# Causal-window attention feeding a mixture of experts: probability-times-V by quadrants, with its output over two PSUM banks and one cycle later

## The chip, the cores and the metric

The kernel runs on one core of a Trainium2 chip. Its time is the device time of one execution in microseconds. Five engines work side by side: TensorE (PE, with its weight loads listed apart as PEld), VectorE (DVE), ScalarE (ACT), GpSimd (POOL) and SyncE (SP), which issues most DMAs. PSUM is the memory that TensorE writes, in banks of 512 fp32 columns by 128 partitions.

## The reference

Eight sequences of 576 tokens with 8 heads of 64 go through attention in a window of 128 keys with a linear bias by head. Each token's 512 numbers then go to the one of eight experts that a gate picks.

```python
scores = scale * np.matmul(q, k.transpose(0, 1, 3, 2))
mask = (rel >= 0) & (rel < window)              # rel = query - key, window = 128
scores = np.where(mask, scores + bias[None], -1000000000.0)
attn = np.exp(scores - np.max(scores, axis=-1, keepdims=True))
attn = attn / (np.sum(attn, axis=-1, keepdims=True) + 1e-09)
x = np.matmul(attn, v)                          # then (B * S, H * D)
expert_idx = np.argmax(x @ w_gate, axis=1)
...
h = np.maximum(xe @ w1[e], 0.0)
out[mask] = gate_w[mask, None] * (h @ w2[e])
```

## The kernel before, in words

**Chunks.** Attention works on 36 chunks of 128 queries: four whole ones per sequence (m = 0 to 3) and, for each pair of sequences, one tail chunk made of the last 64 queries of both. A chunk with m > 0 sees two blocks of 128 keys, its own (kb = 1) and the one ahead (kb = 0). A chunk with m = 0 sees its own alone. In a tail chunk the own block has 64 keys. So there are 8 chunks with m = 0, 24 full ones and 4 tails.

**Steps of a chunk.** `scores` (S0 and S1, four heads each) adds the bias by a matmul and then the products of q and k, in 64*64 tiles of the array. Since each query sees 128 keys of 256, the two halves are folded by `copy_predicated` in `weigh` (F) and ACT takes the exponents (E0; E10 and E11 for the two halves of S1's). `transposes` (T0, T1) turns the probabilities into a bank of `b_ps`. `place` (P0, P1) copies that bank by ACT to `pT` at kb = 1 and then has POOL write kb = 0 and kb = 1 by `affine_select`, which sets to zero what the window leaves out. `av` (V0, V1) multiplies by v into a bank of `b_ps`; `copy_x` (X) copies that by ACT to `xT`. `rows` (R) turns the rows back and takes the gate's products. `scale_rows` (Y) divides by the sum and starts the write to DRAM.

**V.** Each matmul of `av` has a head's 64 columns of v as weights (128 keys) and 128 columns of `pT` as the moving operand. The masked `pT` holds two quadrants of zeros in each full chunk: late keys of the own block for the first 64 queries, and early keys of the block ahead for the last 64. V multiplies them too. Tiles are named rows*columns in the trace: 128*64 for V, and 64*64 for S and R.

**Order.** The order is written by hand. A cycle is four steps of `step(s)`; chunk ch starts at step 4*ch. `PLACES` gives each operation its step and its rank in the step. On PE a cycle is S0 of the newest chunk, T1 and T0 of older ones, R, S1 and V. V at (11, 7) is in the same cycle as T1 and P1 at 8 of its chunk. X stands at (11, 9), R at 16. Chunks outside `SPLIT` (the first ones) take the exponents of S1 in one piece and their sums on DVE (`SUMS`).

**Beside it.** While attention runs, 14 halves of expert weights are rounded to fp32r by ACT (`round_half`, a cast) and their rest is taken by POOL (`rest_half`). `W0` and `W1` say in which cycles, and when the halves are loaded. Loads are spread over slots, `PN` = 5 to a cycle, with a due slot and a first slot for each kind. `route` is a generator: each piece of routing a group of chunks is run at the end of a cycle.

**PSUM.** `ps_s` has four banks for scores, `ps_r` two for R, and `ps_b` two that rotate among T1, T0 and V.

Of the kernel before, what the change touches and what calls it, by code (L numbers as in the profile page):

```python
# [44 lines left out]
def attention(ctx, tc, st, qT, kT, v, iw, load_c2, chunk_done, chunks, begun):  # L45
# [7 lines left out]
    ptp = ctx.enter_context(tc.tile_pool(name="a_pt", bufs=2))  # L53
    xp = ctx.enter_context(tc.tile_pool(name="a_x", bufs=2))
    ps_s = ctx.enter_context(tc.tile_pool(name="ps_s", bufs=1, space=PSUM))
    ps_b = ctx.enter_context(tc.tile_pool(name="ps_b", bufs=2, space=PSUM))
    ps_r = ctx.enter_context(tc.tile_pool(name="ps_r", bufs=1, space=PSUM))
    st["bank"] = bank = lambda: ps_b.tile([128, 4, 128], F32, name="b_ps")
    flat = lambda ap: ap.rearrange("p a b -> p (a b)")
    st["ptp"] = ptp  # L60

# [184 lines left out]
    def av(subs, pT, x_ps, pairs):  # L246
        m, tail = subs[0][1] // 4, is_tail(subs)
        spans = [(subs[2 * a][0], slice(64 * a, 64 * a + 64)) for a in range(2)] if tail else [(subs[0][0], slice(0, 128))]
        whole = [(p, b, q, kb) for p in pairs for b, q in spans for kb in ((0, 1) if m > 0 else (1,))]
        if tail:  # L250
            whole.sort(key=lambda x: x[3])
        for p, b, q, kb in whole:
            kk = 64 if (m == 4 and kb == 1) else 128
            first, last = kb == 0 or m == 0, kb == 1
            if tail:
                first, last = (p, b, q, kb) == whole[0], (p, b, q, kb) == whole[-1]
            for c in range(2):
                h = 2 * p + c
                anchor(nc.tensor.matmul(  # L259
                    out=x_ps[64 * c:64 * c + 64, p, q], lhsT=blocks["v", b, m - 1 + kb][0:kk, D * h:D * h + D],  # L260
                    rhs=pT[0:kk, kb, h, q], start=first, stop=last,
                ))

    def rows(xT):
        st["r_ps"] = r_ps = ps_r.tile([128, 2, 512], F32, name="r_ps")
# [29 lines left out]
                        needs[key].append((j, ch))  # L295
                    uses[key][j] = ch
    wanted = []
    for key, load, have, bufs, free, due in (("q", load_q, 3, QBUF, 3, -2 * PN - LEAD[0]), ("v", load_v, 2, VBUF, 2 * PN + 4, 2 * PN + 3 - LEAD[1])):
# [40 lines left out]

    def copy_x(ch):  # L340
        xTs[ch] = xp.tile([128, NP, 128], F32, name="xT", bufs=3)
        nc.scalar.copy(out=xTs[ch], in_=xps.pop(ch))

    def do(k, ch):
        perform(k, ch)
# [3 lines left out]
    def perform(k, ch):  # L349
# [11 lines left out]
        elif k == "E10":  # L361
            weighed[ch, 1]((0,))
        elif k == "E11":
            weighed.pop((ch, 1))((1,))
        elif k in ("A0", "A1"):
            nc.vector.tensor_reduce(out=sums[ch][:, 4 * g:4 * g + 4], in_=pes[ch][:, 4 * g:4 * g + 4, :], axis=AX.X, op=ALU.add)
            if g:
                guard(sums[ch])
        elif k in ("T0", "T1"):
            if ch not in pTs:  # L370
                pTs[ch] = ptp.tile([128, 2, H, 128], F32, name="pT")
            turned[ch, g] = transposes(g, pes[ch])
# [55 lines left out]
    for s in range(HAND, max(plan) + 1):  # L428
        step(s)


SPLIT = range(3, 36)
SUMS = {0: (2, 6), 1: (4, 6), 2: (6, 6)}
PLACES = dict(S0=(0, 0), T1=(8, 1), E11=(4, 2), T0=(4, 3), P1=(8, 4), P0=(4, 5), R=(16, 6), F0=(0, 7), Y=(16, 8), S1=(0, 9),
              F1=(0, 10), E0=(0, 11), V0=(11, 7), V1=(11, 7.2), X=(11, 9), I=(15, 9.5), E10=(3, 10))
HOOKS = dict(Q=4.5, G=20, round=(2, 2), rest_of=(2, 21))
SLOTS = dict(S0=0, T0=1, S1=2, V0=3, V1=4)
PN = 5
LEAD = (7, 10, 11, 8)
# [113 lines left out]
def route(tc, st, lg, c0, G, groups):  # L553
# [875 lines left out]
```

## Time and profile before

| | us |
|---|---|
| time, median of 3 runs | 627.55 (626.51 to 627.57) |
| the profiled execution, its own time | 626.94 |
| its span, first to last instruction | 625.2 |
| PE busy in the span | 614.3 (98%) |
| attention at its steady pace, 20.86 to 192.42 | 171.56 |
| from there to the first steady expert work at 213.30 | 20.88 |
| the rest, expert work | 411.90 |

The page gives busy time of each engine over the whole span. The view by windows gives it by stretch. The timeline lists what each engine did in order, neighbours of one kind merged: start, length, engine, line, operation, what it writes and reads, the tile of the array, the operands' shape and the count, and in brackets the idle time ahead of it with what ended it. The length of a merged PE row reaches to the end of its last matmul, which overlaps the next row; so the distance between two starts is what a step costs.

### The profile page before, as it was taken

The page shows a single profiled execution, that of the slowest core. Times are in us where ns is not written, and L with a number is a line of the kernel's source. Part 1 is how long each engine was busy: PE and PEld are TensorE (multiplying, and loading weights), DVE is VectorE, ACT ScalarE, POOL GpSimd, SP SyncE. Part 2 cuts the span into 40 slices and gives each one's busy share as a digit, 9 for nine tenths or more (in the row PEclk, how much of TensorE's full clock was granted, in tenths as well). Part 3 has the DMA queues.
Part 4 walks back from the last instruction along what each step waited for, and adds up shares of the span by engine and source line. Part 5 has one row for each costly group of instructions (what it writes and reads, how often), then busy time and mean ns, then how long its engine had stood idle before and what let it go on. Part 6 is the DMA issues. An engine that isn't in the chain of part 4 may idle for free.

```text
span 625.2 us, 16743 instructions
## 1 busy us (share of the span) xinstructions
PE 614.3 (98%) x6544; PEld 527.0 (84%) x6544; DVE 377.0 (60%) x887; ACT 312.7 (50%) x939; POOL 316.6 (51%) x483
## 2 busy tenths in 40 slices
PE   8999999999999999999999999999999999999996
PEld 5888877877878888898989999989999998888885
DVE  6777887877888875535654564565466365455411
ACT  5888888998886324423342333334234333433311
POOL 5646788978664221365247508624751750670302
PEclk9999999999999999999999999999999999999999
DMA  7757978788645256273444425434442642544101
GB/s 272 217 188 232 292 208 270 234 265 258 212 129 181 77 163 213 85 289 113 147 156 120 127 84 178 123 112 144 132 136 77 203 114 68 194 126 139 67 1 62
DMA packets 46995, 100.16 MB, mean 160 GB/s; under 512 B 12149, under 2 KB 12405, under 8 KB 46914
## 3 DMA queue, kind: packets, MB, share of 16 engines
q1 hardware_dynamic: 38434, 77.85, 39.1%
q0 software_dynamic: 8336, 20.96, 11.7%
q8 instruction: 52, 0.85, 0.6%
q10 hardware_dynamic: 144, 0.26, 0.2%
q14 instruction: 29, 0.24, 0.1%
HBM read 78.96 MB, written 20.09 MB: 158 GB/s over the span
## 4 chain that ended last, share of the span: by engine, by line
PE 84%; POOL 7%; ACT 3%; DVE 2%; DMA 2%; issue 1%; POOLq 0%; DVEq 0%; ACTq 0%
PE y_ps L1037 32%; PE l_ps L831 31%; PE b_ps L259 7%; PE s_ps L192 4%; PE b_ps L227 3%; PE r_ps L271 2%; ACT pe L215 2%; POOL pT L243 2%; POOL wl L1154 2%; POOL pT L241 2%; PE s_ps L183 2%; PE s_ps L831 1%; POOL q_sb L86 1%; ACT pT L233 1%; PE x_ps L788 1%
## 5 line engine op out<-in xcount | busy, mean ns | idle before, releaser
L834 ACT ACTIVATE hh<-l_ps 128x320 fp32r<-128x320 f32 (+4 forms) x104 | 46.5, 447 | 200.8 <-PE l_ps L831 200.8
L838 DVE SCALAR_TENSOR_TENSOR hl<-l_ps,hh 128x320 fp32r<-128x320 f32 (+4 forms) x104 | 52.3, 502 | 146.9 <-ACT hh L834 146.6
L811 POOL DMA_INDIRECT xg<-xd,od_idx x112 | 116.4, 1039 | 35.1 <-issue 32.0
L1037 PE MATMUL y_ps<-wh,hh 128*128 128x512 f32 x280 | 109.9, 393 | 0.0
L1025 POOL DMA_INDIRECT out<-y,od_pidx x33 | 34.9, 1057 | 148.0 <-ACT y L1043 141.5
L1037 PE MATMUL y_ps<-wl,hh 128*128 128x512 f32 x280 | 109.4, 391 | 0.0
L1037 PE MATMUL y_ps<-wh,hl 128*128 128x512 f32 x280 | 109.2, 390 | 0.0
L215 ACT ACTIVATE pe<-s_ps,nmax 128x128 f32<-128x128 f32 x288 | 101.7, 388 | 7.0 <-DVE nmax L209 6.7
L1137 DVE TENSOR_TENSOR wl<-w_raw,wh 128x512 fp32r<-128x512 f32 x114 | 73.8, 689 | 31.3 <-ACT wh L1133 30.8
L831 PE MATMUL l_ps<-xh,wh 128*128 128x320 f32 (+8 forms) x416 | 81.0, 316 | 0.0
L831 PE MATMUL l_ps<-xl,wh 128*128 128x320 f32 (+8 forms) x416 | 80.5, 315 | 0.0
L831 PE MATMUL l_ps<-xh,wl 128*128 128x320 f32 (+8 forms) x416 | 80.3, 315 | 0.0
L831 PEld LDWEIGHTS l_ps<-xh,wh 128*128 128x128 f32 x416 | 67.8, 188 | 6.7 <-issue 1.2
L259 PE MATMUL b_ps<-pT,v_sb 128*64 128x128 f32 (+2 forms) x1136 | 66.7, 266 | 1.1 <-POOL pT L243 1.0
L831 PEld LDWEIGHTS l_ps<-xl,wh 128*128 128x128 f32 x416 | 65.9, 188 | 2.0
L831 PEld LDWEIGHTS l_ps<-xh,wl 128*128 128x128 f32 x416 | 65.8, 188 | 2.0
L259 PEld LDWEIGHTS b_ps<-pT,v_sb 128*64 128x64 f32 (+1 forms) x1136 | 56.0, 136 | 12.5 <-POOL pT L241 4.0
L1037 PEld LDWEIGHTS y_ps<-wh,hl 128*128 128x128 f32 x280 | 52.6, 188 | 11.5
L1133 ACT CAST wh<-w_raw 128x1024 fp32r<-128x1024 f32 x57 | 59.5, 1044 | 5.2 <-DMA w_raw<-w 5.2
L1037 PEld LDWEIGHTS y_ps<-wh,hh 128*128 128x128 f32 x280 | 52.6, 188 | 9.6 <-ACT hh L834 0.4
L1037 PEld LDWEIGHTS y_ps<-wl,hh 128*128 128x128 f32 x280 | 52.6, 188 | 9.2
L215 ACT ACTIVATION_READ_ACCUMULATOR pe<-s_ps,nmax 128x1 f32 x264 | 60.0, 227 | 0.0
(241 smaller groups left out, 915.1 us busy)
## 6 DMA issues: line engine op xcount, KB each, us to landing
w_raw<-w SPq DMA_DIRECT2D x56, 512.0 KB, 3.7
q_sb<-qT SPq DMA_DIRECT2D x39, 256.0 KB, 3.7
xd<-x_sb SPq DMA_DIRECT2D x32, 288.0 KB, 3.0
v_sb<-v SPq DMA_DIRECT2D x32, 256.0 KB, 4.4
k_sb<-kT SPq DMA_DIRECT2D x24, 256.0 KB, 3.8
w_raw<-w SPq DMA_DIRECT2D x16, 256.0 KB, 4.1
w_n<-w SPq DMA_DIRECT2D x4, 1024.0 KB, 6.8
k_sb<-kT SPq DMA_DIRECT2D x8, 384.0 KB, 4.2
```

What stands on the lines that cost most here:

```text
L192: anchor(nc.tensor.matmul(out=s_ps[halves(a), c, n, x0:x1].rearrange("p (u x) -> p u x", x=64), lhsT=blocks["q", b, m][h, 2 * g + n, qs], ...
L215: nc.scalar.activation(out=pe[:, h, :], in_=s_ps[:, c, n, lo:lo + 128], func=AF.Exp, bias=nmax[:, 2 * c + n:2 * c + n + 1], scale=1.0, **( ...
L227: anchor(nc.tensor.transpose(out=t_ps[:, j, :], in_=pe[:, 4 * g + j, :], identity=ident))
L259: anchor(nc.tensor.matmul(out=x_ps[64 * c:64 * c + 64, p, q], lhsT=blocks["v", b, m - 1 + kb][0:kk, D * h:D * h + D], rhs=pT[0:kk, kb, h, ...
L811: ins = tc.nc.gpsimd.indirect_dma_start(out=g[:, s], out_offset=None, in_=parts, in_offset=bass.IndirectOffsetOnAxis(ap=idx[:, s], axis=0),)
L831: nc.tensor.matmul(out=ps, lhsT=a[:, 128 * d:128 * d + 128], rhs=b[:, d], start=(k == 0), stop=(k == 11))
L834: nc.scalar.activation(out=hh, in_=ps, func=AF.Relu)
L838: nc.vector.scalar_tensor_tensor(out=hl, in0=ps, scalar=0.0, in1=hh.bitcast(F32), op0=ALU.max, op1=ALU.subtract)
L1025: ins = nc.gpsimd.indirect_dma_start(**kw).ins
L1037: nc.tensor.matmul(out=ys[t], lhsT=a[:, tl], rhs=b[:, 512:1024], start=(f == 0 and k == 0), stop=(f == 7 and k == 2))
L1133: keep(tc, nc.scalar.copy(out=wh, in_=raw))
L1137: keep(tc, eng.tensor_tensor(out=wl[:, sl], in0=raw[:, sl], in1=wh.bitcast(F32)[:, sl], op=ALU.subtract))
```

## The change

- `av` no longer runs whole blocks. `products` lists its matmuls: those on all 128 keys for 64 queries (`every`), and, for the quadrants that remain, those on 64 keys (`top` or `low`). The quadrants of zeros are left out in full chunks. In each full chunk the 64-key ones stand first and last, the 128-key ones between. A chunk with m = 0 leaves no quadrant out.
- The first and the last 64 queries go to different banks of one tile `b_ps` of two banks, 256 columns of each. T1 and T0 take the two banks in turn (`bank`). X reads both banks.
- V and X stand a cycle later, at 15 in place of 11. `pT` gets a third buffer, v an eighth, and v's slots follow. At the end (chunks 32 to 35) V stays earlier.
- Weight halves are rounded from cycle 3 in every second cycle (`W0`, `W1`), not in cycles 14 to 27.
- In `route` the exponent `ex` is issued a piece later. Chunk 2 is split as the later ones are.

```diff
+    b_ps = ps_b.tile([128, 2, 512], F32, name="b_ps")
+    def bank():
+        next_bank[0] ^= 1
+        return b_ps[:, next_bank[0] ^ 1].rearrange("p (a b) -> p a b", a=4)
...
+        def add(rg, g, n, b, kb, q):
+            todo.extend((rg, 2 * g + n, c, (b, m - 1 + kb), kb, q) for c in range(2))
+        def whole(g):
+            for a, (b, q) in enumerate(at):
+                for n in range(2):
+                    add(every, g, n, b, 0 if tail else a if m else 1, q)
+        def rest(g0, g1):
+            for n in range(2):
+                if tail:
+                    for b, q in at:
+                        add(top, g0, n, b, 1, q)
+                elif m > 0:
+                    add(top, g0, n, at[0][0], 1, top)
+                    add(low, g1, n, at[0][0], 0, low)
+        rest(0, 0)
+        whole(0)
+        half = len(todo)
+        whole(1)
+        rest(1, 1)
...
+                out=x_ps[64 * c:64 * c + 64, q.start // 64, p],
+                lhsT=blocks["v", *j][rg, D * h:D * h + D], rhs=pT[rg, kb, h, q],
...
-        nc.scalar.copy(out=xTs[ch], in_=xps.pop(ch))
+        to, x_ps = xTs[ch].rearrange("c p (a q) -> c a p q", a=2), xps.pop(ch)
+        nc.scalar.copy(out=to, in_=x_ps)
...
-SPLIT = range(3, 36)
+SPLIT = range(2, 36)
-              ... V0=(11, 7), V1=(11, 7.2), X=(11, 9), ...
+              ... V0=(15, 7), V1=(15, 7.2), X=(15, 9), ...
-W0 = 14
-W1 = 1
+W0 = 3
+W1 = 2
-VBUF = 7
+VBUF = 8
...
     ex = rp.tile(sh3, F32, name="ex")
-    nc.scalar.activation(out=ex, in_=sh, func=AF.Exp)
     if apart:
         yield
+    nc.scalar.activation(out=ex, in_=sh, func=AF.Exp)
```

On PE, V of a full chunk in the middle of attention, before (`s_ps` are the scores, `b_ps` V's output; Pool waits are those on the masks in `pT`):

```order
L192 MATMUL s_ps<-k_sb,q_sb 64x192 x8
L259 MATMUL b_ps<-pT,v_sb 64x128 [waits Activation_49,Pool_49]
L259 MATMUL b_ps<-pT,v_sb 64x128
L259 MATMUL b_ps<-pT,v_sb 64x128 [waits Pool_49]
L259 MATMUL b_ps<-pT,v_sb 64x128 x5
```

The same place after:

```order
L199 MATMUL s_ps<-k_sb,q_sb 64x192 x8
L292 MATMUL b_ps<-pT,v_sb 64x64 [waits DMAHW7_49,Activation_49]
L292 MATMUL b_ps<-pT,v_sb 64x64 x15
L292 MATMUL b_ps<-pT,v_sb 64x64 [waits Pool_49]
L292 MATMUL b_ps<-pT,v_sb 64x64 x3
L292 MATMUL b_ps<-pT,v_sb 64x64 [waits Pool_49]
L292 MATMUL b_ps<-pT,v_sb 64x64 x11
```

V has 32 matmuls of 64 columns in place of 16 of 128, and its masks are those of the cycle before.

On PE, the transposes behind S0, before (T1 and T0 are four matmuls each):

```order
L192 MATMUL s_ps<-k_sb,q_sb 64x192 x7
L227 MATMUL b_ps<-c_sb,pe 128x128 [waits PE_49]
L227 MATMUL b_ps<-c_sb,pe 128x128 x3
L227 MATMUL b_ps<-c_sb,pe 128x128 [waits Activation_49]
L227 MATMUL b_ps<-c_sb,pe 128x128 x3
L271 MATMUL r_ps<-iw_sb,xT 64x72 [waits DVE_49]
```

And after:

```order
L199 MATMUL s_ps<-k_sb,q_sb 64x192 [waits DMAHW2_49,Pool_49]
L199 MATMUL s_ps<-k_sb,q_sb 64x192 x7
L234 MATMUL b_ps<-c_sb,pe 128x128 [waits Activation_49]
L234 MATMUL b_ps<-c_sb,pe 128x128 x7
L305 MATMUL r_ps<-iw_sb,xT 64x72 [waits DVE_49]
```

T1 waited for no copy of V's output; now the first of the eight waits for ACT, which has to read both banks of X.

On PE, near the end, V of chunk 32 before, with S0 of the last chunk behind it:

```order
L192 MATMUL s_ps<-k_sb,q_sb 64x192 x8
L259 MATMUL b_ps<-pT,v_sb 64x128 [waits DMAHW7_49,Activation_49]
L259 MATMUL b_ps<-pT,v_sb 64x128 x7
L183 LDWEIGHTS eye_sb [waits DVE_49]
L183 MATMUL s_ps<-bias_sb,eye_sb 64x2x192 [waits Activation_49]
```

And after, V of chunk 32 and V of chunk 33:

```order
L199 MATMUL s_ps<-k_sb,q_sb 64x192 x8
L292 MATMUL b_ps<-pT,v_sb 64x64 [waits DMAHW0_49,Activation_49]
L292 MATMUL b_ps<-pT,v_sb 64x64 x15
L292 MATMUL b_ps<-pT,v_sb 64x64 [waits DMAHW2_49,Activation_49,Pool_49]
L292 MATMUL b_ps<-pT,v_sb 64x64 x15
```

The two V now stand directly behind each other, with X of the first between them on ACT.

## Rows read from the trace of the kernel before

**Rows 1.** The page, busy us, share of the span and instructions

```profile
PE 614.3 (98%) x6544; PEld 527.0 (84%) x6544; DVE 377.0 (60%) x887; ACT 312.7 (50%) x939; POOL 316.6 (51%) x483
```

**Rows 2.** By windows: length, busy PE, PEld, DVE, ACT, POOL, clock, DMA share, GB/s

```profile
20.86:192.42 171.56, 168.42 (x3689) 136.36 (x3688) 133.14 (x293) 147.79 (x627) 126.34 (x251) 1.00 0.75 230
...
213.30:625.20 411.90, 406.31 (x2295) 359.54 (x2291) 211.16 (x490) 141.15 (x240) 173.21 (x189) 1.00 0.42 129
```

**Rows 3.** Timeline of PE, one cycle: start, length, what, tile, shape, count

```profile
66.63 0.36 PE L183 MATMUL s_ps<-bias_sb,eye_sb 64*64 64x384 bf16 x4
...
67.57 1.09 PE L227 MATMUL b_ps<-c_sb,pe 128*128 128x128 f32 x8
68.59 0.73 PE L271 MATMUL r_ps<-iw_sb,xT 64*64 64x72 f32 x32
69.14 0.34 PE L183 MATMUL s_ps<-bias_sb,eye_sb 64*64 64x384 bf16 x4
...
70.06 1.97 PE L259 MATMUL b_ps<-pT,v_sb 128*64 128x128 f32 x32
71.96 0.30 PE L183 MATMUL s_ps<-bias_sb,eye_sb 64*64 64x256 bf16 x4
...
72.63 1.09 PE L227 MATMUL b_ps<-c_sb,pe 128*128 128x128 f32 x8
```

**Rows 4.** Timeline of PE, V of a chunk with m = 0

```profile
60.27 1.09 PE L259 MATMUL b_ps<-pT,v_sb 128*64 128x128 f32 x16
61.30 0.36 PE L183 MATMUL s_ps<-bias_sb,eye_sb 64*64 64x384 bf16 x4
```

**Rows 5.** Timeline of PE, V of a tail chunk

```profile
130.03 2.52 PE L259 MATMUL b_ps<-pT,v_sb 128*64 128x64 f32 x64
132.49 0.42 PE L652 MATMUL r_ps<-rr,lp 128*128 128x48 bf16 x10
```

**Rows 6.** Timeline of PE, three V that last longer

```profile
39.74 1.09 PE L259 MATMUL b_ps<-pT,v_sb 128*64 128x128 f32 x16
40.96 0.36 PE L183 MATMUL s_ps<-bias_sb,eye_sb 64*64 64x384 bf16 x4
...
153.46 0.88 PE L259 MATMUL b_ps<-pT,v_sb 128*64 128x128 f32 x12 [0.27 <-POOL pT L243]
...
157.69 1.09 PE L259 MATMUL b_ps<-pT,v_sb 128*64 128x128 f32 x16
158.79 0.36 PE L183 MATMUL s_ps<-bias_sb,eye_sb 64*64 64x384 bf16 x4
```

**Rows 7.** Timeline of ACT and of PE about 101 us

```profile
101.46 0.24 ACT L575 ACTIVATE ex<-sh 128x40 f32<-128x40 f32 x1 [1.31 <-POOL sh L566]
...
102.44 0.36 PE L183 MATMUL s_ps<-bias_sb,eye_sb 64*64 64x384 bf16 x4 [1.01 <-ACT pe L215]
```

**Rows 8.** Timeline of ACT, a cycle without a cast and one with

```profile
66.75 0.58 ACT L342 COPY xT<-b_ps 128x512 f32<-128x512 f32 x1 [0.85 <-PE b_ps L259]
...
68.61 1.09 ACT L233 COPY pT<-b_ps 128x512 f32<-128x512 f32 x2
...
70.84 0.27 ACT L215 ACTIVATION_READ_ACCUMULATOR pe<-s_ps,nmax 128x1 f32 x1
72.08 0.58 ACT L342 COPY xT<-b_ps 128x512 f32<-128x512 f32 x1 [0.97 <-PE b_ps L259]
...
97.83 0.68 ACT L1149 CAST wh<-w_raw 128x512 fp32r<-128x512 f32 x1
98.85 0.59 ACT L342 COPY xT<-b_ps 128x512 f32<-128x512 f32 x1 [0.34 <-PE b_ps L259]
```

**Rows 9.** Timeline of PE and of ACT near the end of attention

```profile
195.24 0.60 PE L227 MATMUL b_ps<-c_sb,pe 128*128 128x128 f32 x4
195.77 1.97 PE L259 MATMUL b_ps<-pT,v_sb 128*64 128x128 f32 x32
...
196.18 0.66 ACT L233 COPY pT<-b_ps 128x512 f32<-128x512 f32 x1
```

More of the change, by code (lines that the diff above doesn't have):

```diff
@@ L52, in attention @@
     pp = ctx.enter_context(tc.tile_pool(name="a_p", bufs=PEB))
-    ptp = ctx.enter_context(tc.tile_pool(name="a_pt", bufs=2))
+    ptp = ctx.enter_context(tc.tile_pool(name="a_pt", bufs=3))
     xp = ctx.enter_context(tc.tile_pool(name="a_x", bufs=2))
     ps_s = ctx.enter_context(tc.tile_pool(name="ps_s", bufs=1, space=PSUM))
-    ps_b = ctx.enter_context(tc.tile_pool(name="ps_b", bufs=2, space=PSUM))
+    ps_b = ctx.enter_context(tc.tile_pool(name="ps_b", bufs=1, space=PSUM))
     ps_r = ctx.enter_context(tc.tile_pool(name="ps_r", bufs=1, space=PSUM))
-    st["bank"] = bank = lambda: ps_b.tile([128, 4, 128], F32, name="b_ps")
+    b_ps = ps_b.tile([128, 2, 512], F32, name="b_ps")
+    next_bank = [0]
+    def bank():
+        next_bank[0] ^= 1
+        return b_ps[:, next_bank[0] ^ 1].rearrange("p (a b) -> p a b", a=4)
+    st["bank"] = bank
     flat = lambda ap: ap.rearrange("p a b -> p (a b)")
@@ L244, in place, with products @@
                                     channel_multiplier=-1, compare_op=ALU.is_ge, fill=0.0)
-    def av(subs, pT, x_ps, pairs):
+    def products(subs):
         m, tail = subs[0][1] // 4, is_tail(subs)
[L248 to L262, printed above, removed]
+        todo = []
+        top, low, every = slice(0, 64), slice(64, 128), slice(0, 128)
+        at = [(subs[2 * a][0], q) for a, q in enumerate((top, low))]
+        def add(rg, g, n, b, kb, q):
[17 more added lines that the diff above has]
+        rest(1, 1)
+        return todo, half
@@ new lines, in av @@
+    def av(subs, pT, x_ps, part):
+        todo, half = products(subs)
+        ends = {}
+        for i, (_, p, c, _, _, q) in enumerate(todo):
+            ends.setdefault((q.start, c), []).append(i)
+        for i, (rg, p, c, j, kb, q) in enumerate(todo):
+            if (i >= half) != part:
+                continue
+            h = 2 * p + c
+            anchor(nc.tensor.matmul(
+                out=x_ps[64 * c:64 * c + 64, q.start // 64, p],
+                lhsT=blocks["v", *j][rg, D * h:D * h + D], rhs=pT[rg, kb, h, q],
+                start=i == ends[q.start, c][0], stop=i == ends[q.start, c][-1],
+            ))
@@ L297, in attention @@
     wanted = []
-    for key, load, have, bufs, free, due in (("q", load_q, 3, QBUF, 3, -2 * PN - LEAD[0]), ("v", load_v, 2, VBUF, 2 * PN + 4, 2 * PN + 3 - LEAD[1])):
+    for key, load, have, bufs, free, due in (("q", load_q, 3, QBUF, 3, -2 * PN - LEAD[0]), ("v", load_v, 2, VBUF, 3 * PN + 4, 3 * PN + 3 - LEAD[1])):
         for n, (j, ch) in enumerate(needs[key]):
@@ L376, in perform @@
             if g == 0:
-                xps[ch] = bank() if ch else ps_r.tile([128, 2, 512], F32, name="r_ps")[:, 0].rearrange("q (p x) -> q p x", p=NP)
-            av(subs, pTs[ch], xps[ch], range(2 * g, 2 * g + 2))
+                xps[ch] = (b_ps if ch else ps_r.tile([128, 2, 512], F32, name="r_ps"))[:, :, 0:256].rearrange("c a (p q) -> c a p q", p=NP)
+            av(subs, pTs[ch], xps[ch], g)
         elif k == "X":
@@ L429, in attention @@
         step(s)
-SPLIT = range(3, 36)
-SUMS = {0: (2, 6), 1: (4, 6), 2: (6, 6)}
+SPLIT = range(2, 36)
+SUMS = {0: (2, 6), 1: (4, 6)}
 PLACES = dict(S0=(0, 0), T1=(8, 1), E11=(4, 2), T0=(4, 3), P1=(8, 4), P0=(4, 5), R=(16, 6), F0=(0, 7), Y=(16, 8), S1=(0, 9),
-              F1=(0, 10), E0=(0, 11), V0=(11, 7), V1=(11, 7.2), X=(11, 9), I=(15, 9.5), E10=(3, 10))
+              F1=(0, 10), E0=(0, 11), V0=(15, 7), V1=(15, 7.2), X=(15, 9), I=(15, 9.5), E10=(3, 10))
 HOOKS = dict(Q=4.5, G=20, round=(2, 2), rest_of=(2, 21))
@@ L453, in places @@
         at.update(V0=(7, 7), X=(12, 0.5))
-    if ch in (4, 13, 22, 31):
-        at["V0"] = (9, 7)
+    if ch == 32:
+        at.update(V0=(14, 7), V1=(14, 7.2), X=(14, 9))
+    if ch not in SPLIT:
+        at.update(V0=(11 if ch else 7, 7), V1=(11, 7.2))
     if ch > 32:
@@ L458, in places @@
         at.update(I=(r, 2.9), R=(r, 3), Y=(r, 3.1), V0=(v0, 7), V1=(v1, 8))
-        if ch > 33:
-            at["X"] = (v1, 8.1)
+        at["X"] = (v1, 8.1 if ch > 33 else 9)
         if ch == 35:
```

## The prediction, made before the changed kernel had run

> **What bounds the kernel now.** I read the shares of busy time first, then the busy time of three stretches, then TensorE's order of work in single cycles, and last what it waits for. TensorE (PE) is busy for 98% of the span [rows 1]. That is an average over two programs, so the stretches count: in the attention part PE is busy 168.42 of 171.56 us at a granted clock of 1.00, ScalarE (ACT) 147.79, and in the expert part PE 406.31 of 411.90 [rows 2]. The change touches attention alone; the expert part I leave as it is. One attention cycle shows no gap: S0 at 66.63, the transposes T at 67.57, R at 68.59, S1 at 69.14, V at 70.06, the next S0 at 71.96 [rows 3]. A cycle is 5.33 us, and V is 1.90 of it. Whatever V gives back on PE shortens the cycle, as long as ACT, with 86% of the same time, keeps up.
>
> **Price of a V record.** The trace shows each fp32 matmul as two records. A full V has 32 of 128 columns and takes 1.90 us to the next S0 [rows 3]; V of a chunk at the start of a sequence has 16 and takes 1.03 [rows 4]. The difference, 0.87 us for 16 records, gives 54.4 ns for a record of 128 columns, and 0.16 us that do not grow with the records. I read the 0.16 as the price of changing the array's tiling, since R to S1, both in 64*64 tiles, needs no such time. V of a tail chunk has 64 records of 64 columns in 2.46 us [rows 5]; by the code its tiles alternate 128*64, 64*64, 128*64, 64*64, so four changes, 0.64, go off: 28.4 ns for a record of 64 columns, with two column tiles working at once. Half the columns cost half the time. For four 64*64 tiles at once the row is R: 32 records of 72 columns in 0.55 us, 17.2 ns each [rows 3]; at 64 columns I take 16.
>
> The Trainium skill ("TensorEngine Tiling (Array Packing)", Instruction Overhead) says that each matmul has about 60 cycles of overhead, and that one should not take the tiling factor from a dimension that is already small. Read as a surcharge of 25 ns on each added record, shared by two column tiles, a full V would pay about 0.4 us more (an estimate from that page), and the gain below would be gone. The trace disagrees: 28.4 ns is 1.2 ns more than half of 54.4.
>
> **V after, part by part.** A full V (24 chunks) becomes 16 records of 64x64 before, 32 of 128*64 in the middle, and 16 of 64x64 behind. Before, the streams take 32 x 54.4 = 1.74 us; after, 32 x 28.4 + 32 x 16 = 1.42. Tiling changes stay two: they stood at V's entry and exit, they now stand inside V, because S1 ahead and S0 behind are 64*64 like V's ends. Gain 0.32; with R's unscaled 17.2 it is 0.28. I take 0.30: 24 x 0.30 = 7.2 us. A chunk at the start of a sequence (8) leaves no quadrant out and halves its columns: 32 x 28.4 - 16 x 54.4 = +0.04 each, +0.3 us. A tail chunk (4) keeps 64 records in two column tiles but has three changes instead of five, counting entry and exit: 4 x 2 x 0.16 = 1.3 us gained. Sum: **8.2 us** less on PE, between 7.5 and 9.
>
> **V a cycle later.** Before, V follows the transposes, the copies P and the two POOL masks of the same cycle. In ten cycles this is too late: the first of them lasts 1.22 from V to S0 instead of 1.03, the last 1.10, and between them one stands at 153.46 behind POOL's mask [rows 6]. The excess of the ten over 1.90 and 1.03 is 3.2 us. A whole cycle more, and POOL's weight differences in every second chunk only, clears them: **3.2 us** gained, at least 2.
>
> **The route's exponent a step later.** At 101.46 ACT has stood 1.31 us for POOL's subtraction, and PE pays 1.01 of it at 102.44 [rows 7]. Issued a step later it finds its input ready: **1.0 us** gained.
>
> **New waits: X in front of T.** X now reads both banks that T writes, V fills both, and V waits for the copies P0 out of them. Before, X begins 0.12 us after S0 and lasts 0.58 [rows 3, 8]; behind an end in 64*64 tiles, which S0 overlaps, I estimate 0.2 to 0.3 after S0, so the banks are free at 0.8 to 0.95. T stands 0.94 behind S0 of a full chunk, which hides the wait, but 0.67 behind S0 of a chunk at a sequence's start [rows 3]: 0.2 us each. In those cycles PE's way to V is shorter by two such differences, while ACT needs 2.95 us from X to the end of P0 (66.75 to 69.70) [rows 8]: another 0.2. Six such cycles: **+2.4 us**, between 0.6 and 3.6.
>
> **The weight halves.** ACT has 0.85 to 0.97 us idle ahead of X without a cast, and 0.34 with one [rows 8]. V's 0.30 comes off that. The 14 casts remain, in every second cycle now, each followed by a cycle with room; where the cycle is a short one X is late by 0.1 to 0.2. I take **+1.0 us**, 0 to 2.5. POOL and the DMA queues get the same bytes earlier and more evenly. The DMA share of 0.75 [rows 2] covers that; if a q or v load slips, its chunk waits, which I price in the range only.
>
> **Filling.** With V from chunk 2 on a cycle later, the fifth cycle has no V and is 1.9 us shorter on PE. ACT's own work from X to the end of E0 is 4.36 us (66.75 to 71.11) [rows 8], so PE waits at S0 or S1, while the V not done there is paid at the end. I take **+1.2 us**, 0.5 to 1.9.
>
> **Draining.** At the end T, V and X follow each other with little between. Four places wait for one ACT copy each, since there is no other bank pair: V of chunk 33 behind X of 32 (0.12 + 0.58, by estimate 0.75 with the signals), T behind X of 33 (0.6), V of 34 behind the copy of T's last bank, which ACT begins at 196.18 and ends at 196.84 where V now starts at 195.77 [rows 9] (0.8 after T's own delay), and the route's matmuls behind X of 35 (0.7). **+2.85 us**, 1.5 to 3.5.
>
> The third pT buffer, the eighth v buffer and the sums of chunk 2 taken on ACT only make room, or move two reductions off DVE (133.14 us busy in the attention part, less than ACT [rows 2]): nothing.
>
> **Sum.** 8.2 + 3.2 + 1.0 = 12.4 us gained, 2.4 + 1.0 + 1.2 + 2.85 = 7.45 lost: 4.95. The profiled execution took 626.94 us with a span of 625.2; 622.0 would be its own figure, and at the median of 627.55, 0.6 above it, **622.6**.
>
> **Rivals.** (1) ACT sets the pace, and the kernel is slower. Place: X, queued behind E0 and the cast. Price: X late in every cycle, T waits 0.45 us in 31 cycles, 14 us, of which 3.4 are in the sum: 633. It decides from some 0.2 us per cycle, where the 4.95 is used up. For it: ACT needs 4.36 us per cycle, with a cast some 0.5 more (the idle time ahead of X falls from 0.85 to 0.34), and PE's cycle falls to 5.03. Against it: the idle time ahead of X [rows 8] and that casts alternate. The Trainium skill ("TensorEngine Tiling (Array Packing)", PSUM Bottleneck) warns of just this: tiling speeds up TensorE but not the copies out of PSUM. No row of before shows ACT setting the pace for longer than one cycle. (2) The 64x64 ends run two at a time, not four: 32 records at 28.4 instead of 16 ns, 24 x 0.40 = 9.5 us, **632**. Against it: R's 17.2 ns [rows 3]. (3) The change doesn't win what it says because many small waits of 0.1 to 0.2 us take it: 627. (4) The new waits are mostly covered, losses of 2 us only: **617**.
>
> **How the numbers follow.** Forecast (619 to 626): 0.58. Rival 4: 0.15. Rival 3: 0.14. Rival 1: 0.09. Rival 2: 0.04. This kernel's measurement tells 0.2%, 1.25 us, from no change. Faster is the forecast, rival 4 and half of rival 3, 0.80; within 0.2%, 0.08; slower the rest, 0.12. The range reaches from rival 4 to rival 3 with its upper edge, 617 to 627.5, and leaves rivals 1 and 2 and the edges out, some 0.18.
>
> **What would show it.** Right: the full V takes about 1.7 us to S0 with records of 64 columns, no [POOL pT] wait stands at V, S0 follows S0 after about 5.0 us, the largest new waits stand at T behind X and in the last 20 us of attention, and the expert part keeps its length. Wrong: V near 1.9 or above (records do not overlap), a wait of T for xT in every cycle, or DMA waits at S or V early on.

## The result: slower by 0.9%, and the profile after

The changed kernel takes **632.55 us** (median of 4 runs, 631.72 to 635.48); the kernel before took 627.56 beside it. The ratio is 1.0088, 95% interval 1.0063 to 1.0112. The forecast was 622.6 and faster; the range ended at 627.5. The profiled execution has a span of 630.1 us, 4.9 more than before. One later run of the changed kernel took 1195.69 us and is left out of every time and ratio below.

The page and the view by windows, to set beside [rows 1, 2] (busy time of PE, PEld, DVE, ACT, POOL, clock, DMA share, GB/s):

```profile
PE 609.8 (97%) x7440; PEld 529.2 (84%) x7440; DVE 377.3 (60%) x885; ACT 314.0 (50%) x947; POOL 316.9 (50%) x483
...
20.64:192.45 171.81, 164.55 (x4489) 138.48 (x4480) 134.70 (x296) 149.04 (x629) 126.39 (x250) 1.00 0.72 228
192.45:214.36 21.91, 20.26 (x384) 18.89 (x385) 16.91 (x73) 9.72 (x31) 4.13 (x7) 1.00 0.27 82
214.36:630.10 415.74, 408.35 (x2304) 360.71 (x2300) 211.12 (x490) 141.47 (x240) 173.24 (x189) 0.99 0.41 129
```

Attention at its steady pace takes 171.81 us where it took 171.56; PE's busy time there fell by 3.9, so PE now waits 7.3 us in place of 3.1. The end of attention takes 1.03 more. The largest difference, **3.84 us**, stands where the prediction expected none: in the expert part, whose code the change does not touch, 415.74 in place of 411.90.

One attention cycle, PE's timeline, as [rows 3] of before:

```profile
30.48 0.34 PE L190 MATMUL s_ps<-bias_sb,eye_sb 64*64 64x384 bf16 x4
...
31.40 1.09 PE L234 MATMUL b_ps<-c_sb,pe 128*128 128x128 f32 x8
32.42 0.73 PE L305 MATMUL r_ps<-iw_sb,xT 64*64 64x72 f32 x32
32.98 0.34 PE L190 MATMUL s_ps<-bias_sb,eye_sb 64*64 64x384 bf16 x4
...
33.79 1.88 PE L292 MATMUL b_ps<-pT,v_sb 64*64 64x64 f32 x64
35.49 0.34 PE L190 MATMUL s_ps<-bias_sb,eye_sb 64*64 64x384 bf16 x4
```

V now takes 35.49 - 33.79 = 1.70 us to the next S0, and S1 to V 0.81 in place of 0.92: together 2.51 for 2.82. The cycle is 5.01 us for 5.33. That is the quadrants' gain as forecast, 0.31. So the question is where the rest went. What PE waited for in the whole execution (us, times, longest):

```profile
PE s_ps L190 <- ACT pe L222: 3.4, 5, 1.1
PE b_ps L234 <- ACT xT L377: 2.3, 6, 0.8
PE x_ps L824 <- DMA xg<-xd,idx: 2.1, 1, 2.1
...
PE b_ps L292 <- POOL pT L248: 1.6, 2, 0.8
PE b_ps L292 <- issue: 0.9, 2, 0.6
...
PE r_ps L688 <- DVE rr L682: 0.7, 2, 0.6
```

Three of these lines were not in the sum: the wait of the expert part for the gathered rows xg, V waiting for "issue" (nothing that the profile shows), and part of S0's wait for ACT (0.43 at 159.98; the rest stands in the first 26 us, where the pipeline fills).

### The profile page after: what moved, and what is told of

It reads as the page before. It is cut to its first block, busy times and chain, and to the rows that moved or that the text cites. A ratio compares the mean times of both kernels' runs of the same rounds, so it can differ in the third digit from the quotient of the medians.

```text
span 630.1 us, 18546 instructions
## 1 busy us (share of the span) xinstructions
PE 609.8 (97%) x7440; PEld 529.2 (84%) x7440; DVE 377.3 (60%) x885; ACT 314.0 (50%) x947; POOL 316.9 (50%) x483
## 4 chain that ended last, share of the span: by engine, by line
PE 87%; ACT 6%; DVE 3%; DMA 1%; issue 1%; POOL 1%; POOLq 0%; DVEq 0%; ACTq 0%
PE y_ps L1073 32%; PE l_ps L867 31%; PE b_ps L292 8%; PE s_ps L199 5%; PE b_ps L234 4%; ACT pe L222 4%; PE r_ps L305 3%; PE s_ps L190 2%; PE s_ps L867 1%; ACT xT L377 1%; ACT pT L240 1%; DVE nmax L216 1%; PE x_ps L824 1%; DMA xg<-xd,idx 1%; DVE s_ps L213 1%
## 5 line engine op out<-in xcount | busy, mean ns | idle before, releaser
L292 PE MATMUL b_ps<-pT,v_sb 128*64 128x64 f32 (+1 forms) x2016 | 63.9, 226 | 2.7 <-POOL pT L248 1.6
L222 ACT ACTIVATION_READ_ACCUMULATOR pe<-s_ps,nmax 128x1 f32 x272 | 62.0, 228 | 0.0
```

The source lines that it names most:

```text
L222: nc.scalar.activation(out=pe[:, h, :], in_=s_ps[:, c, n, lo:lo + 128], func=AF.Exp, bias=nmax[:, 2 * c + n:2 * c + n + 1], scale=1.0, **( ...
L292: anchor(nc.tensor.matmul(out=x_ps[64 * c:64 * c + 64, q.start // 64, p], lhsT=blocks["v", *j][rg, D * h:D * h + D], rhs=pT[rg, kb, h, q], ...
```

## Where the expert part lost 3.84 us

The first y starts 1.08 us later than before (214.37 for 213.29). Then PE stands for 2.05 us behind a y matmul, PE's timeline:

```profile
221.45 0.66 PE L824 MATMUL x_ps<-c_sb,xg 128*128 128x128 f32 x4 [2.05 <-DMA xg<-xd,idx]
```

and afterwards it works at 1.2 GHz, half its clock, for some four microseconds (windows of 1 us):

```profile
222.00:223.00 1.00, 1.00 (x5) 0.81 (x5) 0.19 (x1) 0.59 (x1) 0.00 (x0) 0.83 0.83 189
223.00:224.00 1.00, 1.00 (x4) 0.76 (x3) 1.00 (x4) 0.00 (x0) 0.00 (x0) 0.50 0.68 116
...
226.00:227.00 1.00, 1.00 (x12) 0.56 (x11) 0.54 (x1) 0.43 (x1) 0.69 (x2) 0.96 0.93 377
```

A y matmul then comes every 0.42 us in place of 0.23. Matched by their place in the program, the y and l matmuls are 1.08 us late at the first y, 3.22 after the wait, 4.93 after the slow stretch, and 4.94 at the end: wait 2.1, clock 1.7, nothing else.

Why is xg late? POOL's view names DVE as the gather's releaser. But DVE had written the index at 215.6, and the gather also waits for every write into `xd`. The last of them is the gate's, line L717. SP's timeline, and for that one write the time from issue to landing (us):

```profile
208.45 2.09 SPq L717 DMA_DIRECT2D xd<-gate  x4
210.65 0.42 SPq L1017 DMA_DIRECT2D w_n<-w  x1
211.25 0.37 SPq L717 DMA_DIRECT2D xd<-gate  x1
...
DMA to landing us min/median/max: 5.1/5.1/5.1
```

and what waits for it on POOL:

```profile
217.13 1.60 POOL L815 DMA_INDIRECT xg<-xd,idx  x1 [18.66 <-DVE e_hl L873]
```

`w_n` is a load of 1 MB; it lands at 216.23, the half kilobyte of gates behind it at 216.39, and the gather starts at 217.13. In the kernel before `w_n` was issued at 187.23, and the gate's write landed 1.7 us after its issue. The order of SP's instructions shows what moved, and what `w_n` waits for:

```order
L91 DMA v_sb<-v 128x512 [waits DMAHW3_49,PE_49]
L981 DMA w_n<-w 128x4x512 [waits DMAHW4_49,PE_49]
```

before, and after:

```order
L717 DMA xd<-gate_4854 128x3x1 [waits DMAHW6_49,DMAHW7_49,DMAHW1_49,DMAHW0_49]
L1017 DMA w_n<-w 128x4x512 [waits DMAHW2_49,PE_49,Activation_49]
L717 DMA xd<-gate_4938 128x1 [waits DVE_49]
```

`w_n` now waits for ACT as well, so something that the end of attention still writes has to be done first. The third pT buffer and the eighth v buffer changed the layout of the memory; that `w_n` shares bytes with one of them is inferred from this wait, not shown. In before_cols, before_ex and before_halves `w_n` still stands right behind a load of v, so neither the number of matmuls nor those two edits moved it.

## Stands of PE at block borders

The gap named "issue", PE's timeline (V of a full chunk, 64 records, then the route's matmuls):

```profile
126.47 1.77 PE L292 MATMUL b_ps<-pT,v_sb 64*64 64x64 f32 x56
128.82 0.34 PE L292 MATMUL b_ps<-pT,v_sb 64*64 64x64 f32 x8 [0.59 <-issue]
```

V stops before its last 8 records. By the order no wait stands there. Counted along PE's instructions in the trace (matmuls, weight loads and the few others), the record after the gap is number 6337 = 24 x 256 + 193. The gap at 177.40 is at 8897 = 34 x 256 + 193, and S0 at 122.78, which lasts 1.31 to T in place of 0.92, stops at 6081 = 23 x 256 + 193. The DMA queue of kind "instruction" brings PE's program in pieces of 16 KB; between 30 and 190 us it brought (queue, kind: pieces, MB, share) before

```profile
q8 instruction: 27, 0.44, 1.1%
```

and after

```profile
q8 instruction: 34, 0.56, 1.5%
```

A piece lasts some 256 PE instructions. V by quadrants has twice the matmuls (7440 records for 6544 in the whole kernel), so PE uses up a piece in 4.7 us in place of 5.9. At the borders with a stand the newest piece had landed 1.1 to 1.6 us ahead; in the kernel before no border comes within 2.4 us of a landing, and none has a stand of over 0.2. Not every border so close behind a landing has a stand: record 4801 comes 1.5 us behind one and has none. In the changed kernel these stands take 0.39 + 0.81 + 0.51 + 0.22 = 1.9 us.

## The experiments

The first 20 us of a profile, in which the first tiles are loaded, vary by over 2 us between profiles even of one kernel (the steady pace begins at 20.64 in one profile of the changed kernel and at 23.12 in another), and the chips differ. So beside the ratio I give two stretches of each profile, from the first S0 of the steady pace to the first y, and from there to the end. Before, they are 213.29 - 20.86 = 192.4 and 411.9.

| kernel | ratio to before (95%) | S0 to first y | first y to end |
|---|---|---|---|
| changed, first chip | 1.0088 (1.0063 to 1.0112) | 193.7 | 415.7 |
| after_again | 1.0094 (1.0064 to 1.0125) | 194.5 | 414.3 |
| gate_first | 1.0066 (1.0040 to 1.0091) | 195.3 | 414.9 |
| gate_first_2 | 1.0055 (1.0033 to 1.0076) | 194.6 | 412.6 |
| v_old_place | 1.0084 (1.0052 to 1.0115) | 197.0 | 414.9 |
| all_quadrants | 1.0136 (1.0106 to 1.0166) | 198.7 | 414.9 |
| before_cols | 1.0089 (1.0056 to 1.0123) | 197.9 | 413.6 |
| before_ex | 0.9985 (0.9964 to 1.0007) | 191.6 | 411.8 |
| before_halves | 0.9993 (0.9973 to 1.0013) | 192.1 | 411.8 |
| ex_after_x | 1.0066 (1.0046 to 1.0085) | 192.6 | 412.7 |
| halves_late | 1.0093 (1.0062 to 1.0124) | 193.2 | 412.6 |
| before_ex_halves | 0.9981 (0.9966 to 0.9996) | 191.2 | 411.9 |
| no_quadrants | 0.9999 (0.9982 to 1.0016) | 191.1 | 411.8 |

**gate_first and gate_first_2: the w_n load behind the gates.** The load waits for PE's first transposes of the late gathered rows.

```diff
-            behind(tc, r, st["quiet"])
+            behind(tc, r, st["turned"][2])
...
+    st.setdefault("turned", []).append(r.ins)
```

> The changed kernel with one load moved: the 1 MB load w_n waits for the first transposes of the gathered rows, so that it can no longer stand between the last gate write and its landing. My theory: the expert part is 3.8 us longer only because in the changed kernel w_n is issued on SP at 210.65 and the last gate write, issued at 211.25 behind it, lands at 216.39 in place of 1.7 us after its issue; the first gather of xg waits for that write, PE then waits 2.05 us for xg and works some 5 us at half clock. Expected: the last gate write lands within 2 us, no wait of over 0.5 us at the transposes of xg, granted clock 1.00 through the expert part, everything ahead of 210 us as in the changed kernel: 628.7 us. Rival: the gather is late for DVE (the profile names e_hl as its releaser) or because attention ends later; then the time stays at 632.

It ran once beside three others (634.1 us; before took 629.58 on that chip) and once beside the changed kernel, which took 633.01 there (median of three).

> The changed kernel unchanged, beside the next run, on the chip of these four. Both theories: 5 us slower than before if this chip supplies PE's instructions as the first one did; 6 to 8 if it does so as the chip of the first four experiments (which lost 1.5 us more at block borders). The wait for xg after a late gate write (2 us) and the half clock behind it are there again.

> The kernel with the w_n load moved once more, so that it is compared with the changed kernel on one chip. My theory: the last gate write lands 1.7 us after its issue, and from the first y to the end it is 3 us shorter than the changed kernel; the times 3 us apart. Rival: what the trace shows there is given back, and the times are within 1 us.

Beside each other, 633.01 became 630.54: 2.5 us, where 3 were expected. SP's timeline of gate_first_2, the landing of the last gate write, and PE at the transposes of xg:

```profile
209.59 3.12 SPq L717 DMA_DIRECT2D xd<-gate  x5
221.59 0.38 SPq L1018 DMA_DIRECT2D w_n<-w  x1
...
DMA to landing us min/median/max: 1.4/1.4/1.4
...
220.85 0.66 PE L824 MATMUL x_ps<-c_sb,xg 128*128 128x128 f32 x4 [0.55 <-DMA xg<-xd,idx]
```

The expert part has 412.6 us, 3.1 less than the changed kernel's first profile and 1.7 less than after_again, and the clock is 1.00. In after_again the wait of 2.1 us is there again, but not the half clock (1.00 from 217.58 to 232), and 414.3 remains: so the wait is the queue's, while the slow clock followed it in one profile of two. The theory holds; the 0.7 us left over before is mostly the wait of 0.55. The first run of this kernel shows 414.9 because PE stands for 1.7 us about 278 to 279 us, at a place in the expert part where v_old_place and all_quadrants stand too; the cause of that is open, and before_cols, which has none of the change's other edits, stands for 1.0 at another place. Its attention was also slow: a stand of 1.34 us at 126.33, again at record 6081. So the 628.7 expected was missed, and the chip, on which the kernel before is 2.0 us slower too, makes part of that.

**before_cols: twice the V matmuls without anything else.**

```diff
-        spans = ... if tail else [(subs[0][0], slice(0, 128))]
+        spans = ... if tail else [(subs[0][0], slice(64 * a, 64 * a + 64)) for a in range(2)]
```

> The kernel before with one edit: V of chunks other than tails in halves of 64 columns, the same work in twice as many matmuls (896 more PE matmul records, the number that the change added). Price without anything else: a full V of 64 records at 28.4 ns plus 0.16 is 1.98 us in place of 1.90, 24 of 0.08 and 8 of 0.04: 2.2 us, 629.8. My theory on top of it: PE's instructions come in blocks of 16 KB over the DMA rings (a block for about 252 PE instructions), and with more instructions per microsecond blocks come just in time; PE then stands without any releaser at a few block borders, 1 to 2 us in all: 631. Rival: the stands in the changed kernel at 123.3, 128.8 and 177.4 have another cause; then none such here and 629.8 or less.

Measured 635.32 against 629.58, 5.7 us more, above both. V of a full chunk takes 2.02 to S0, 0.12 more than before, which makes 3.3 with the other chunks. The rest are stands, PE's timeline:

```profile
79.86 0.27 PE L192 MATMUL s_ps<-k_sb,q_sb 64*64 64x128 f32 x1 [0.52 <-issue]
...
185.75 0.55 PE L192 MATMUL s_ps<-k_sb,q_sb 64*64 64x192 f32 x6 [0.64 <-issue]
...
202.34 0.22 PE L271 MATMUL r_ps<-iw_sb,xT 64*64 64x72 f32 x1 [0.33 <-issue]
```

They fall on records 3521, 8897 and 9665, each 193 over a multiple of 256, and in S, S and R, not in V (a smaller one, 0.23 at record 3265, is in V). The kernel before has none. So the stands belong to the number of PE's instructions, not to quadrants, banks or the place of V. In all later kernels with V in 64 columns they are there again at the same remainder, 0.9 to 3 us in a run; in those without, one of 0.3 at most.

**all_quadrants: the same instructions, zeros included.**

```diff
-                    add(every, g, n, b, 0 if tail else a if m else 1, q)
+                    if tail:
+                        add(every, g, n, b, 0, q)
+                    else:
+                        for kb in (0, 1) if m else (1,):
+                            add(every, g, n, b, kb, q)
...
-                elif m > 0:
-                    add(top, g0, n, at[0][0], 1, top)
-                    add(low, g1, n, at[0][0], 0, low)
```

> The kernel with the w_n load moved, in which a full chunk multiplies the quadrants of zeros too: 32 matmuls of 128*64 with 64 columns in place of 16 of 64*64 and 16 of 128*64, as many instructions as before. My theory (price of a record: 28.4 ns in 128*64 tiles, 16 in 64*64): V of a full chunk takes 1.97 us to S0 and S1 to V 0.92, in place of 1.70 and 0.81, less where a cycle waits for ACT anyway: 18 chunks of 0.4 and 6 of 0.2, 8 us more than the kernel with the load moved, 637. Rival: ACT sets the pace of attention already, and what V is shorter is waited for elsewhere; then half of it or less, 633 or below.

638.21 against 634.1 of gate_first on the same chip: 4.1 us, half of the forecast and so the rival's number. PE's timeline of a full cycle:

```profile
59.55 0.34 PE L190 MATMUL s_ps<-bias_sb,eye_sb 64*64 64x384 bf16 x4
...
60.48 2.08 PE L293 MATMUL b_ps<-pT,v_sb 128*64 128x64 f32 x64
62.49 0.36 PE L190 MATMUL s_ps<-bias_sb,eye_sb 64*64 64x384 bf16 x4
```

V has 2.01, and S1 to V 0.93: 0.43 more than the 1.70 and 0.81 of the quadrants, as the prices say. So the rival's reason, ACT setting the pace, does not hold there. The 0.43 falls on cycles in which nothing else is late. In cycles with an S0 of a chunk at a sequence's start the difference is 0 to 0.26, and some cycles lost a stand at a border that gate_first had, about 1 us together. The price of a record holds; of what is won on PE about half shows between these two kernels.

**v_old_place: V back in its old cycle.**

```diff
-              ... V0=(15, 7), V1=(15, 7.2), X=(15, 9), ...
+              ... V0=(11, 7), V1=(11, 7.2), X=(11, 9), ...
```

> The kernel with the w_n load moved, and V and X back in the cycle in which they stood before (step 11), the end of attention as before; quadrants and the two banks stay. My theory: a cycle later cost about 2 us where the pipeline fills (PE has one V less to do but ACT sets the pace there) and some 3.4 us where it drains, and gave back the 3.2 us of waits for POOL's masks. Expected: waits of V for pT return in about ten cycles, 3 to 4 us in all; cycles of 4.9 us from 20 us on; V 33 and V 34 no longer behind X and the masks; 626 to 627 us. Rival: V at its old place meets POOL's masks in every cycle, because X in front of T moves T, P and the masks by 0.2 to 0.3 us while V itself stands 0.1 us earlier; 30 cycles of 0.2 to 0.4 us more, 631 or above.

v's slots and the place of chunk 32 go back with it; the first half of a tail's V, which stood at 9 before, stands at 11. 634.58 for gate_first's 634.1; neither number. The waits for masks return, in this V twice, PE's timeline:

```profile
153.65 0.45 PE L292 MATMUL b_ps<-pT,v_sb 128*64 128x64 f32 x8 [0.17 <-POOL pT L248]
154.36 0.84 PE L292 MATMUL b_ps<-pT,v_sb 128*64 128x64 f32 x24 [0.26 <-POOL pT L250]
```

and T waits for X 2.4 us in 8 places. So by the times a cycle later is worth nothing that can be measured with the quadrants, though in the profile the stretch to the first y is 1.7 us longer without it: what the masks' waits cost is about what the fill and the drain cost.

**no_quadrants: all but the quadrants and the two banks.**

```diff
-    ps_b = ctx.enter_context(tc.tile_pool(name="ps_b", bufs=1, space=PSUM))
+    ps_b = ctx.enter_context(tc.tile_pool(name="ps_b", bufs=2, space=PSUM))
...
-            av(subs, pTs[ch], xps[ch], g)
+            av(subs, pTs[ch], xps[ch], range(2 * g, 2 * g + 2))
```

> All of the change but the quadrants and the two banks (V in whole blocks of one bank, as before), with the w_n load moved: V and X a cycle later, three pT buffers, halves from cycle 3, the exponent a piece later. Theory: all waits of V for masks go (3.2 us) and that of the exponent (1.0); the later V costs some 2 us where the pipeline fills and 1 where V 33 stands behind X 32; T waits for no X and PE's instructions are as few as before, so no stands at block borders: 1 to 2 us less than before, about the same as the run before this one. Rival, the prediction's sum without quadrants (3.2 + 1.0 gained, 1.2 and 0.75 lost): 2.3 us less than before. Against both: if the new places themselves make the loss, 2 us more than before.

The cut is against gate_first; `av`, the bank and the copy X are those of before. 626.76 against 627.31, ratio 0.9999. No V waits for a mask any more, and T for X only 0.2 us; what is left is mostly the fill, and 1.2 us for the route's `rr` (PE's waits):

```profile
PE s_ps L183 <- ACT pe L215: 1.9, 3, 0.8
...
PE b_ps L227 <- ACT xT L342: 0.2, 1, 0.2
```

Its stretch to the first y is 191.1; gate_first_2, which differs by the quadrants and the two banks alone, has 194.6. Cycle by cycle, the quadrants win 0.3 in plain cycles and in those with a tail's V, 0.1 to 0.2 where the route's matmuls stand behind V, 3.8 us in all. They lose 2.2 to 2.5 in stands at borders, about 2 where T or S0 waits for X or ACT, and 2.6 at the end of attention, where one tile of two banks makes T, V and the route's matmuls wait for each copy. That is 3.0 to 3.3 more, for 3.5 measured between these two profiles, which are of two chips; the two ratios, 1.0055 and 0.9999, are as far apart.

**before_ex, before_halves, before_ex_halves: the two edits without quadrants.**

```diff
-    nc.scalar.activation(out=ex, in_=sh, func=AF.Exp)
     if apart:
         yield
+    nc.scalar.activation(out=ex, in_=sh, func=AF.Exp)
...
-W0 = 14
-W1 = 1
+W0 = 3
+W1 = 2
```

> The kernel before with one edit: the route's exponent a piece later. The prediction's term: the wait of 1.31 us on ACT and of 1.01 on PE at 102.44 goes, 1.0 us less than before. Rival: the wait goes to another place (the exponent of the 48-column group still waits for POOL's subtraction, as at 161.12 of the changed kernel), where T does not wait for X and nobody pays: still 1.0 less. If instead the DVE and POOL steps behind it come later and hold V or the ranks, no gain.

> The kernel before with one edit: weight halves rounded in every second cycle from cycle 3, as in the changed kernel. Theory: the ten V of before that wait for POOL's masks stand in cycles in which POOL also takes a weight difference (1.27 us); with one in every second cycle half of these waits go, 1 to 2 us less than before. Rival: ACT has less room in the first cycles and the casts hold E and the next S0 there, or the load of the halves delays q and v: no gain or 1 us more.

> The kernel before with the two edits that need no quadrants: the exponent a piece later and the weight halves in every second cycle from cycle 3. Alone they took 1.0 us of waits on PE away (the wait at 102.44) and about 1.5 of the 3.2 us at POOL's masks, the latter losing 1.0 to a wait for the exponent at 77.65, which the former removes. Expected: 2 us less than before, ratio 0.9968. Rival: the waits move to S0 behind ACT's casts in the first cycles, and no more than 0.5 us is left.

The exponent alone: 626.72 for 627.70, its interval includes 1. In the profile the wait of 1.01 is gone, and the cycle, 6.90 us before, has 6.14: V behind it is now 0.23 late for a mask. The halves alone, 626.99: no measurable difference; what V lasts over 1.90 and 1.03 falls from 3.1 to 2.0, the cycle at 165.05 takes 6.39 where before had 5.71, and the exponent's wait returns elsewhere:

```profile
77.65 0.30 PE L183 MATMUL s_ps<-bias_sb,eye_sb 64*64 64x256 bf16 x4 [0.89 <-ACT pe L215]
```

Both together: **625.75 for 627.31, ratio 0.9981** (0.9966 to 0.9996), by the ratio 1.2 us less than before where 2 were expected. It is the only version whose interval lies below 1, and only just; of three such kernels, that is a weak result.

**ex_after_x: the exponent behind X.**

```diff
-PACE = {21: (120, 122, 124, ...
+PACE = {21: (120, 123, 124, ...
```

> The kernel with the w_n load moved and one more edit: the route's exponent of the 48-column group stands a step later, so that X goes ahead of it on ACT. My theory: at 161 us T waits 0.80 us for X, and X for that exponent, which waits 1.19 us for POOL's subtraction: a wait that the prediction took for removed and that the two banks of X hand on to PE. Expected: that T waits 0.2 at most, the cycle of 6.54 us falls to 5.7, 0.8 us less than the kernel with the w_n load moved (which was 2.9 to 4.5 over before). Rival: S0, T and R there wait for ACT's exponents anyway, and the 0.8 comes back within the same cycle.

ACT's and PE's timelines of the kernel with the exponent in front, at the place in question (from the changed kernel):

```profile
161.12 0.24 ACT L613 ACTIVATE ex<-sh 128x48 f32<-128x48 f32 x1 [1.19 <-POOL sh L602]
161.26 0.57 ACT L377 COPY xT<-b_ps 128x512 f32<-128x512 f32 x1
...
161.88 1.09 PE L234 MATMUL b_ps<-c_sb,pe 128*128 128x128 f32 x8 [0.80 <-ACT xT L377]
```

630.61 for 627.31. With the edit, T's wait is gone, but the cycle falls from 6.54 us to 6.33 only: the rank matmuls behind S1 then wait 0.7 us for DVE's x_sb. The rival was right that the gain comes back within the cycle, though by DVE and not by ACT's exponents. The prediction's gain at 102 is real, and the same wait of ACT cost PE nothing in the kernel before (1.12 us at 164.44, in a cycle of 5.71).

What makes DVE late stands a cycle ahead, and it comes from the halves. POOL's timeline and DVE's of the changed kernel, then DVE's of halves_late (below), where no weight difference stands there:

```profile
155.04 1.27 POOL L1190 TENSOR_TENSOR wl<-w_raw,wh 128x512 fp32r<-128x512 f32 x1 [0.29 <-ACT wh L1185]
155.18 1.81 DVE L682 TENSOR_TENSOR rr<-eq,c_sb 128x288 bf16<-128x288 f32 x2
...
159.36 0.78 DVE L682 TENSOR_TENSOR rr<-eq,c_sb 128x288 bf16<-128x288 f32 x2
```

Beside POOL's last weight difference DVE's two `rr` take 1.81 us, without it 0.78. So it is in before_halves too, which has neither quadrants nor the exponent's edit: 1.85, and its next cycle has the 6.39 for 5.71. With the halves in their old places the cycle of 6.54 takes 6.13, and the one ahead, where the route's matmuls wait for `rr`, 4.92 in place of 5.48: 1.0 us together. So of the loss at 161 some 0.4 belongs to the halves' new places, the other 0.4 over before's 5.71 to the exponent ahead of X.

**halves_late: one cast in each of the cycles 14 to 27.**

```diff
-W0 = 3
-W1 = 2
+W0 = 14
+W1 = 1
```

> The kernel with the w_n load moved, with the weight halves rounded as before, one in each cycle from 14 to 27. The prediction gave the casts 1.0 us as they stand and expected X late wherever one stands ahead of it. Theory: with a cast in every cycle X is late by 0.1 to 0.2 in 14 cycles, of which 0.1 reaches T in the full ones: 1 to 2 us more than the kernel with the w_n load moved; the cycles from 20 to 60 us are 0.5 shorter. Rival: the casts have room and T does not wait: within 0.5. The number of PE instructions is the same, so the stands at block borders should be there again, in other places where the halves' loads fill the DMA rings.

632.12, but the stretch to the first y has 193.2 us, 1.4 less than gate_first_2, of which the borders make 1.1; the first 20 us of this profile were 3.5 longer. The two cycles about `rr` make 1.0, and other cycles give 0.7 back, most of it (5.12 for 4.68, at 143.33) where a cast now stands ahead of X in a cycle with a short S0. The plain cycles are 5.01 us with and without a cast. So the casts have room on ACT there, against my theory. The time is 1.5 us above ex_after_x on the same chip, as the theory had it, but in the profile the excess lies in the start; whether the edit makes the start longer is open.

## Why the prediction was wrong, step by step

- **The expert part, "I leave as it is": wrong, 3.84 us.** The step costed the third pT and the eighth v buffer at nothing because they "only make room". With them, by inference from what it waits for, moved the 1 MB load behind which the last gate write stands on SP's queue. The order of SP would have shown this before the run. It is the largest miss; the experiment returns 3.1 of it in the profile, 1.7 against after_again and 2.5 of the time.
- **Price of a V record: right.** 28.4 and 16 ns gave 1.70 us for a V, 2.01 with zeros included and 2.02 in before_cols (1.98 forecast). The row behind it was read loosely: that V of a tail ends at a 128*128 matmul, one that ends at S0 takes 2.19 (no_quadrants), and the step takes off four tiling changes where the tails' term counts five; that 28.4 holds is shown by the two runs with 64 such records. The Trainium skill ("TensorEngine Tiling (Array Packing)", Instruction Overhead) says that each matmul has about 60 cycles of overhead. Read as a surcharge on every matmul, this doesn't show in V's records (2.02 for 1.90 with twice as many), so on that reading the trace disagrees. But doubling the matmuls did have a price, in another place:
- **Stands at block borders, 1.9 us: not in the sum.** I counted PE's records by their duration and not by their number. No view of before shows a stand, but its page has the instruction queue and its pieces.
- **V's sum, 8.2: too large by about 2.** Plain cycles have the 0.31, and tails their 0.30. In the cycles with route matmuls behind V the 64*64 end meets a 128*128 tiling, V takes 1.82 to them and not 1.70 (0.8 in all); I had let the tiling changes stay two everywhere. In the seven cycles with a short S0, where S1 is short too, V wins 0.12 and not 0.30: without any wait such a cycle, at 139.70, takes 4.68 for 4.80 (some 1.2 in all).
- **Masks, 3.2: right** in the steady part. The two V that the list names behind a mask stand in the end of attention, and for the first, at 189.81, POOL had finished at 189.21 and X ended at 189.70: it waited for X.
- **X in front of T, 2.4: right in its place, somewhat high.** In four of the seven cycles with a short S0 T comes 0.24 to 0.34 late and V 0.11; those without other work take 5.01 to 5.12 in place of 4.80. With smaller waits elsewhere that is about 1.7. The largest single wait there, 0.80, came by the exponent (above).
- **The exponent, 1.0: half right.** It was won at 102.44, and about 0.6 was lost again at 161, where before's cycle of 5.71 less the 0.15 that V wins there would be 5.56 and halves_late, without the late DVE, has 6.13.
- **Casts, 1.0: about right in size, by another mechanism.** X behind a cast costs 0.1 to 0.2 at a few S0. The rest is POOL's part, which the step put at nothing ("earlier and more evenly"): its last difference stands beside DVE's `rr`, 1.0 us by halves_late.
- **Filling, 1.2 (0.5 to 1.9): too low.** The first two cycles take 9.84 us with one V, and took 9.69 with two. PE stands 0.47 at T for X and 1.09 at S0 for ACT's exponents, PE's timeline:

```profile
22.10 1.09 PE L234 MATMUL b_ps<-c_sb,pe 128*128 128x128 f32 x8 [0.47 <-ACT xT L377]
...
25.76 0.30 PE L190 MATMUL s_ps<-bias_sb,eye_sb 64*64 64x256 bf16 x4 [1.09 <-ACT pe L222]
```

  The whole 1.9 was lost: the bound's end, not its middle.
- **Draining, 2.85 (1.5 to 3.5): right in its four places, a little low (3.27).** V of 33 starts 0.95 late behind X of 32 (0.75 forecast), T 0.66 behind X of 33 (0.6), V of 34 at 196.49 behind the copy that ends at 196.38, 0.9 (0.8), the route's matmuls 0.76 behind X of 35 (0.7). PE's timeline of the last two:

```profile
196.49 1.94 PE L292 MATMUL b_ps<-pT,v_sb 64*64 64x64 f32 x64 [0.83 <-POOL pT L248]
...
203.17 0.31 PE L688 MATMUL b_ps<-rr,lp 128*128 128x48 bf16 x6 [0.76 <-ACT xT L377]
```

- **The rivals.** ACT setting the pace came near in time (633) and is not what happened: plain cycles are 5.01 us, and T waits for X in 6 places, not 31. ACT does set the pace in the fill. The 64x64 pieces do run four at a time. Small waits (rival 3) are part of it.

The sum: forecast -4.95, measured +4.9 on the profiled span. Of the 9.85 between them, 3.84 are the expert part, 1.9 the borders, about 2 V's smaller win, 0.7 the fill, 0.4 the drain, 0.6 the exponent's new place and 0.3 the halves; X's waits cost about 0.7 less than forecast. About 0.8 is not assigned. The terms in attention are read from cycles of single profiles, good to some 0.1 each.

## What to carry to other kernels

A buffer more can change the memory's layout and with it what a load has to wait for: look in the order of every DMA queue for transfers that moved, and for a small write that now stands behind a large load while somebody waits for it. Where a change splits matmuls, count the instructions per microsecond as well as their durations. Where work on one engine moves, look at what now stands beside it on the others: here a cast moved, and POOL's work behind it slowed DVE's. And what a matmul saves counts only in cycles in which nothing but TensorE is late; sum it over those, not over all.

## What the runs showed of the hardware

- PE's program comes by DMA in pieces of 16 KB, some 256 instructions as the trace counts them. At 4.7 us for a piece, with the DMA engines about 0.73 busy, PE stood 0.2 to 1.4 us at some borders; at 5.9 us at one border in five kernels, 0.3 us. What makes a piece late was not tried.
- A write of 512 bytes behind a load of 1 MB on one queue landed after 5.1 us, and after 1.4 to 2.3 without it.
- A wait of 2.05 us on PE was followed once by some four microseconds at half clock (1.2 GHz), which cost 1.7 us, and once, 2.1 us long at the same place, by none.
- Two `rr` on DVE (128x288, two inputs) took 1.81 us beside a TENSOR_TENSOR on POOL and 0.78 without it.
